# A gated recurrence with two dense layers on one core: all tasks in a new order, with 43 matmuls of zeros in place of 68

## The chip, the cores and the metric

One core of a Trainium2 chip runs the whole program in one launch. The metric is device time in microseconds, the median of the runs of the kernel: 453.35 us over 3 runs (452.59, 454.88 and 453.35). Engines are named as in the profile: PE is TensorE (PEld its weight loads), DVE VectorE, ACT ScalarE, POOL GpSimd, and SP is SyncE, whose queue issues the DMAs.

## What is computed

The first part is a recurrence over 768 steps for 2 x 8 heads of size 40, the second two dense layers of 1536 hidden columns over all 1536 tokens. Cut to its core:

```python
for t in range(S):
    m_new = np.maximum(f_gate[:, :, t] + m, i_gate[:, :, t])
    f_stab, i_stab = np.exp(f_gate[:, :, t] + m - m_new), np.exp(i_gate[:, :, t] - m_new)
    C = f_stab[..., None, None] * C + i_stab[..., None, None] * np.einsum('bhd,bhe->bhde', vt, kt)
    n = f_stab[..., None] * n + i_stab[..., None] * kt
    y[:, :, t] = sigmoid(o_gate[:, :, t]) * (C @ qt) / np.maximum(np.abs(n @ qt), 1.0)
x = y.transpose(0, 2, 1, 3).reshape(1536, 320)
x = (sigmoid(x @ w_gate) * (x @ w_val)) @ w_out
return ((x @ w_a) * (x @ w_b)) @ w_out2
```

## The kernel before, in words

The recurrence is cut into 12 steps of 64 time positions. A step s is a handful of tasks: kq and kv load its data (SP), E0 and E1 are two matmuls of the decay exponents (line 369) into a bank of the pool "e", X0 and X1 their Exp (ACT, L376), S the scores (L399, L414), P0 and P1 their product with the decays (DVE, L424), k0 and k1 the weighted keys (DVE or POOL, L379), ST and st the state sum (L433) and its copy (ACT), O the output sum (L443), N and M its normalisation, D, T, xh and xl the transposed copy of the result, split in a high and a low part, which the first layer reads. The output gate takes a Sigmoid (sg, ACT, L337), which needs another activation table than Exp.

Weights come as 24 blocks (w0 to w23, 960 KB each). Each is made narrow by na (ACT, L216 and L217), nb (DVE, L223), ns, nc and nd, and split by s1 (ACT), s2 (L256) and s3 (DVE or POOL).

The layers are cut into 84 units of one block of 128 hidden columns each. Units 0 to 23 work on 256 tokens and run between the steps of the recurrence; units 24 to 83 work on 512 tokens. A unit is ma and mb (its two products with the input, PE), ga_ (the activation, ACT, L598), gm (their product, DVE, L603), gh_ (ACT, L609) and gl_ (DVE, L614), which split it, and mm and mn, its product with the output weights (PE). In a wide unit ma is 8 pairs of matmuls of 512 columns side by side, mb 7 pairs, and mm and mn 6 pairs of 320 columns each (mm1_half and mm2_half, issued on line 549).

Four units make a segment: their mm and mn add to four sums, one for each 128 tokens, each in a PSUM bank of its own. Two of the banks are the whole pool "acc", two the whole pool "y" (BUFS, line 744), so the next segment's first mm must wait until the old sums are taken out by the four tasks ev (unit_evac: L700 on ACT, L702 and L704 on DVE). The first mm begins with the pair of the first sum of "acc" and the first of "y", and comes to the other two after three pairs. pick (line 899) gives the new sums their banks in the order in which the ev tasks of the old ones stand. In wide segments the four ev tasks read as evK.S, with K the segment and S the sum's block of 128 tokens; the first two of the four are of "acc", the last two of "y".

Nothing is reordered by a program: PLAN (from line 67) names all 1,298 tasks, and line 910 issues them in that order, so each engine runs its own tasks strictly in it. A letter behind a colon chooses the engine (V is DVE, G POOL, A ACT). A star and a number puts so many matmuls of zeros (fill, lines 169 to 172: 512 columns) on PE just ahead of the task: up to ma0 into a bank held for that, afterwards into the next bank that is taken. Waits are left to semaphores.

Of the kernel before, what the change touches and what calls it, by code (L numbers as in the profile page):

```python
# [73 lines left out]
P04 ma1 s12 M3:G k14:G gc2 gp0 D3 mb1 xl2 gm0 s32:G S5 T3 k04:V E05 st3 kv5 gh_0 xh3 O4 xl3 ga_1 X05 ST4 ma2  # L74
N4 pl3 s22:G E15 na3 gp1 P05 k05:G X15 w4 gm1 kq7 gl_0:V M4:V gh_1 mb2 nb3 ga_2 P15 ns3 gp2 ma3 k15:G st4 mb3
E16 gm2 gl_1:G mm0 kv7 nc3 X16 mm1 E07 E06 ma4 ga_3 ev0.0:V ev0.1:V nd3:V gh_2 X06 gp3 mb4 S6 E17 X07 D4 s13
gm3 S7 og2 ST5 O5 na4 k16:V gh_3 X17 P16 P06 gl_2:G k06:G nb4 mm2 s23:V N5 st5 ga_4 s33:G q17:V gp4 gl_3:G P07
ns4 pl4 mm3 sg2 gm4 ma5*1 k17:G mb5 M5:G nc4 O6*1 ST6 kv8 ev1.3:V P17 E18 ma6 ga_5 D5 ev1.2:V mb6 X18 E08
nd4:G gh_4 T5 X08 gp5 ma7 T4 gl_4:V gm5 xh5 kq8 gh_5 gl_5:G ga_6 q07:V mm4 xl5 xh4 N6 mb7 gp6 xl4 w5 st6 kv9
gm6 E19 mm5 kq9 S8 q18:G M6:G k18:G ev2.0 k07:V O7 ga_7 ST7 gh_6 gp7 P18 gm7 D6 na5 P08 N7 ma8 mb8 E09 ma9  # L80
gl_6:G nb5 ns5 ev2.1 nc5 X19 st7 gh_7 q08:G ga_8 M7:G gl_7:G mm6 gp8 T6 mb9 s14 nd5:V ma10 D7 mm7 gm8 s34:G
k08:G X09 T7 xh6 s24:V xh7 kq10 pl5 mb10 ev3.2 xl7 w6 q19:V ga_9 gh_8 gl_8:G q09:G k09:G s15 O8 S9 gp9 xl6 gm9
ev3.3 ST8 P19 N8 P09 ga_10 gh_9 st8 E111 ma11 mm8 mb11 gp10 k19:V O9 na6 ST9 E110 gm10 kq11 M8:G gl_9:G N9
ga_11 ma12 mm9 X110 gh_10 kv11 gp11 gl_10:V M9:V X111 D8 s35:V D9 gm11 nb6 mb12 E010 kv10 X010 k110:V ma13 T9
ga_12 mb13 gh_11 st9 s25:G mm10 T8 xh9 q010:V gp12 w7 gl_11:G gm12 xl9 xh8 ga_13 k010:V gp13 ma14 mm11 gh_12
ev4.4:A ev4.5:A mb14 gm13 gl_12:V q110:G ma15 xl8 ns6 ga_14 nc6 mm12 S11 gp14 gh_13 ST10 gm14 nd6:V P111 E011
gh_14 gl_13:G X011 mb15 ga_15 P011 q011:G st10 mm13 ma16 q111:V gp15 s16 S10 P010 P110 gm15 O11 gl_14:V mb16
N11 gh_15 ga_16 na7 O10 gp16 N10 mm14 ma17 mb17 M11:G D11 gm16 M10:V gl_15:V ma18 D10 s26:V gh_16 T11 mm15
ga_17 T10 mb18 gp17 xh11 gm17 gh_17 gl_16:G ma19 xh10 s36:V ev5.7:V ev5.6:A mb19 ga_18 xl11 mm16 xl10 gp18
gm18 gl_17:G mm17 ga_19 gh_18 ma20 k011:V gl_18:G nb7 mb20 gp19 ns7 gm19 nc7 ma21 gh_19 mm18 ga_20 gl_19:V  # L90
mb21 mm19 gp20 gm20 nd7:V ga_21 ma22 mb22 gh_20 gp21 gl_20:G gm21 w8 ma23 ev6.8:A gh_21 ga_22 gl_21:V ev6.9:V
gp22 gm22 s17 mb23 mm20 ga_23 na8 gh_22 gp23 gm23 mm21 s27:G ma24 s37:V nb8 ma25 mb24 mb25 gh_23 ns8 gl_23:G
# [5 lines left out]
s110 ma35 s310:G gh_32 mb34 ev9.7 s210:G ev9.4 na11 gh_33 ev9.5 gl_32 mm32 mb35 ga_34 mn32 nb11 ns11 gl_33
mm33 nc11 gm34 ga_35 gh_34 gm35 nd11:G gl_34 ma36 ma37 w12 mn33 s111 mm34 mb36 mn34 na12 nb12 ns12 s311:G mb37
s211:G gh_35 ga_36 gl_35 mm35 w13 nc12 gm36 ma38 ga_37 gm37 mn35 gh_36 mb38 nd12:V ev10.10 gl_36 ev10.9 ma39  # L100
ev10.8 gh_37 s112 s212:G ga_38 ev10.11 gm38 gl_37 mm36 na13 ma40 mn36 nb13 mm37 mb39 gh_38 mb40 mn37 gl_38
# [16 lines left out]
ma64 mn61 mb64 ga_63 nb21 gl_62 gm63 ma65 ns21 s120 nc21 gh_63 mm62 ga_64 gl_63 mb65 s320:V mn62 s220:G gm64  # L118
nd21:G ga_65 s121 gh_64 mm63 ma66 mn63 mb66 gm65 gl_64 s221:G ma67 ga_66 ev17.0 ev17.1 s321:G gm66 gh_65
ev17.2 ev17.3 w22 mm64 gl_65 na22 ma68 mn64 mb67 mm65 ga_67 mb68 gh_66 nb22 gm67 ma69 w23 mn65 ns22 gl_66 mm66  # L120
mb69 ga_68 gh_67 gl_67 nc22 nd22:G ga_69 gm68 gm69 mn66 mm67 ma70 mn67 gh_68 na23 ev18.4 ev18.5 gl_68 mb70
ma71 ga_70 ev18.7 ev18.6 gh_69 s122 nb23 mm68 gl_69 ns23 s222:V mb71 mn68 mm69 gm70 s322:V nc23 gh_70 ma72
# [910 lines left out]
```

## Time and profile before

| | |
|---|---|
| median of 3 runs | 453.35 us |
| the profiled execution | 453.09 us |
| its span, first to last instruction | 451.3 us |
| mean granted TensorE clock | 0.993 |
| PE busy, weight loads busy | 430.8 us, 395.0 us |
| DVE, ACT, POOL busy | 299.4, 261.5, 124.4 us |
| moved by DMA | 39.55 MB |

Busy times are unions of instructions. Matmul records are pipelined and their ends modelled, so a busy PE may still be held up for a short while; a wait is only seen as idle time of PE behind the modelled end.

### The profile page before, as it was taken

To read this page: it belongs to the slowest core of one execution; us is meant where nothing else is said; L and a number is where in the kernel's file an instruction comes from. 1 tells how busy PE (TensorE), PEld (TensorE's weight loads), DVE (VectorE), ACT (ScalarE), POOL (GpSimd) and SP (SyncE) were. 2 spreads that over 40 slices of the span, in tenths; PEclk is the share of its full clock that TensorE was granted. 3 is DMA by queue.
4 is the path that set the end of the run, shared out by engine and by line. 5 is a ranking of instruction groups with operands and counts; after the bars stand their busy time and mean duration, and the time that the engine had idled before them with its cause. 6 is when DMAs were issued, how large, how long until landed. Compare 5 with 4: busy or idle time off the path is not lost.

```text
span 451.3 us, 12061 instructions
## 1 busy us (share of the span) xinstructions
PE 430.8 (95%) x5116; PEld 395.0 (88%) x5116; DVE 299.4 (66%) x507; ACT 261.5 (58%) x471; POOL 124.4 (28%) x124
## 2 busy tenths in 40 slices
...
GB/s 223 286 235 295 81 197 285 99 126 63 82 8 89 7 84 18 93 155 1 73 104 56 34 88 1 89 89 1 89 89 1 97 80 2 1 1 2 1 60 116
DMA packets 10470, 39.55 MB, mean 88 GB/s; under 512 B 1840, under 2 KB 3760, under 8 KB 10416
## 3 DMA queue, kind: packets, MB, share of 16 engines
...
q10 hardware_dynamic: 288, 0.33, 0.2%
q14 instruction: 14, 0.11, 0.1%
...
## 4 chain that ended last, share of the span: by engine, by line
PE 82%; ACT 6%; DVE 6%; DMA 2%; issue 1%; POOL 1%; DVEq 0%; SPq 0%; ACTq 0%; POOLq 0%
PE acc L549 21%; PE pa L549 20%; PE pb L549 19%; PE pa L526 8%; PE sp L414 2%; DMA Y<-in_kv_dram 2%; PE o L443 2%; PE acc L533 1%; PE first L172 1%; PE st L433 1%; PE acc L535 1%; PE acc L534 1%; PE e L369 1%; DVE x2tok L704 1%; ACT gh L609 1%
## 5 line engine op out<-in xcount | busy, mean ns | idle before, releaser
L549 PE MATMUL pb<-xb,W 64*128 64x512 f32 x900 | 211.4, 379 | 0.0
L549 PE MATMUL pa<-xb,W 64*128 64x512 f32 x900 | 209.6, 379 | 0.0
L549 PEld LDWEIGHTS pa<-xb,W 64*128 64x128 f32 x900 | 162.9, 187 | 6.0 <-issue 0.2
L549 PEld LDWEIGHTS pb<-xb,W 64*128 64x128 f32 x900 | 163.5, 187 | 4.8
L549 PE MATMUL acc<-W,gh 64*128 64x320 f32 x960 | 108.5, 300 | 7.6 <-DVE x2tok L704 4.4
L549 PEld LDWEIGHTS acc<-W,gh 64*128 64x128 f32 x960 | 93.7, 186 | 13.2 <-DVE x2tok L704 6.1
L609 ACT ACTIVATE gh<-g 128x512 fp32r<-128x512 f32 (+1 forms) x84 | 47.4, 566 | 65.4 <-PE acc L549 54.0
L549 PE MATMUL acc<-W,gl 64*128 64x320 f32 x480 | 84.1, 297 | 0.0
L603 DVE TENSOR_TENSOR g<-g,pb 128x512 f32<-128x512 f32 x60 | 41.0, 687 | 60.1 <-ACT g L598 59.8
L598 ACT ACTIVATE g<-pa 128x512 f32<-128x512 f32 x60 | 35.7, 595 | 71.3 <-PE pa L549 68.8
L614 DVE TENSOR_TENSOR gl<-g,gh 128x512 fp32r<-128x512 f32 (+1 forms) x68 | 47.7, 704 | 42.5 <-ACT gh L609 42.3
L549 PEld LDWEIGHTS acc<-W,gl 64*128 64x128 f32 x480 | 58.8, 187 | 0.1
L256 POOL TENSOR_TENSOR W<-wst,W 128x832 fp32r<-128x832 f32 x14 | 28.7, 2050 | 100.0 <-ACT W L250 77.1
L526 PE MATMUL pa<-xb,W 128*128 128x256 f32 x384 | 48.7, 278 | 0.3 <-DVE ge L659 0.3
L526 PEld LDWEIGHTS pa<-xb,W 128*128 128x128 f32 x384 | 46.1, 192 | 1.2 <-DVE ge L659 0.6
L216 ACT ACTIVATE cva<-wst 128x960 f32<-128x960 f32 x24 | 31.5, 1311 | 6.0 <-DMA wst<-in_w_dram 2.6
L234 DVE SCALAR_TENSOR_TENSOR cva<-wst,cva 128x960 int32<-128x960 int32 x24 | 33.1, 1378 | 0.3
L704 DVE SCALAR_TENSOR_TENSOR x2tok<-acc,x2tok 128x320 f32<-128x320 f32 x52 | 22.9, 483 | 13.0 <-PE acc L549 12.8
L240 POOL TENSOR_TENSOR wst<-cva,wst 128x960 int32<-128x960 int32 x7 | 16.6, 2371 | 51.7 <-DVE cva L234 33.4
L217 ACT ACTIVATE wst<-wst 128x960 int32<-128x960 uint32 x24 | 30.6, 1276 | 0.0
L250 ACT ACTIVATE W<-wst 128x832 fp32r<-128x832 f32 x24 | 26.4, 1102 | 1.2 <-POOL wst L240 0.6
L614 POOL TENSOR_TENSOR gl<-g,gh 128x256 fp32r<-128x256 f32 x16 | 17.3, 1086 | 31.1 <-ACT gh L609 22.7
...
## 6 DMA issues: line engine op xcount, KB each, us to landing
...
rhsE<-V SPq DMA_DIRECT2D x24, 2.0 KB
```

The source lines that it names most:

```text
L216: nc.scalar.activation(cva[0], hi.bitcast(F32), AF.Abs)
L217: nc.scalar.activation(lo, lo.bitcast(U32), AF.Copy, scale=2.0**-29)
L234: nc.vector.scalar_tensor_tensor(ai, hi, -0x40000000, ai, op0=ALU.bitwise_and, op1=ALU.bitwise_or)
L250: nc.scalar.activation(w[:, 0:NH], g[:, 0:NH], AF.Copy)
L256: e.tensor_tensor(w[:, NH : 2 * NH], g[:, 0:NH], w[:, 0:NH].bitcast(F32), op=ALU.subtract)
L526: nc.tensor.matmul(dst, w[:, w0 : w0 + P], x[:, h, cb].rearrange("p a b -> p b a"), start=(i == 0), stop=(i == 7))
L549: last = [nc.tensor.matmul(o, w, x, start=st, stop=sp) for o, w, x, st, sp in pair]
L598: nc.scalar.activation(t, pa, AF.Copy if l else AF.Sigmoid)
L603: nc.vector.tensor_tensor(t, t, pb, op=ALU.mult)
L609: nc.scalar.activation(gh, g, AF.Copy)
L614: eng.tensor_tensor(gl, g, gh.bitcast(F32), op=ALU.subtract)
L704: nc.vector.scalar_tensor_tensor(dst[:, 0:DM], acc, half, dst[:, 0:DM], op0=ALU.mult, op1=ALU.add)
```

## The change

Only PLAN differs. The same 1,298 tasks stand in another order. The matmuls of zeros go from 68 (E00*25 S0*4 E01*5 S1*4 ST0*5 E14*3 T0*5 S3*7 O2*4 ST2*4 ma5*1 O6*1) to 43 (S0*14 E01*2 E11*2 S1*4 E02*5 E13*6 ST0*1 S3*3 ST2*3 ST4*1 E08*2). Some tasks change their engine: of k0 and k1 five go from DVE to POOL net, of nd three; one of gl_; two of M, two of the q tasks, one pr and one half of a split (s2 or s3) go from POOL to DVE net; and of the ev tasks three from ACT to DVE. In the queue of SP kq1 now stands ahead of kv0 and og0, and kv3 ahead of kv2. The lines of the diff around the start and around eight of the segments' ends:

```diff
-start yz0 cst lhs0:A ga0 gb0 gd0 rhs1:A ge0 gl1 ga1 rhs0:A yi0:A gc0 gb1 w0 pr0:V na0 E00*25 gd1 pr1:V nb0 E10
-X10 kq0 kv0 ge1 lhs1:A X00 og0 kq1 sg0 w1 ns0 k10:V gc1 S0*4 E11 yz2 yz1 gl2 pr3:G kq2 E01*5 nc0 X11 kv1 k00:G
-P10 P00 S1*4 X01 kq3 kv2 pr2:V E12 O0 X12 yi1:A nd0:V P01 P11 pr4:V ST0*5 E02 pr5:G E03 k11:G na1 S2 X02 k01:G
-st0 ga2 N0 nb1 og1 M0:V s10 P12 s30:G s20:V yi2:A k12:G k02:G w2 P02 O1 E13 ns1 ST1 N1 X03 nc1 gb2 X13 D0 M1:V
-nd1:V E14*3 T0*5 S3*7 kv3 st1 X14 sg1 kq4 gd2 kv4 kq6 k13:G k03:G P03 xh0 D1 P13 kq5 O2*4 s11 ST2*4 T1 na2 xl0
-s21:V E04 S4 st2 O3 N2 s31:G nb2 xh1 ge2 ST3 P14 w3 kv6 xl1 ma0 ns2 M2:G D2 X04 N3 nc2 T2 mb0 nd2:V xh2 ga_0
...
-gl_27 nb9 w10 mm26 mb29 mn26 ns9 mm27 nc9 ga_29 gm28 gm29 gh_28 ma30 mn27 nd9:V gh_29 na10 ma31 mb30 gl_29
-gl_28 ev8.0 ev8.3 ev8.2 nb10 ev8.1 s19 ga_30 ns10 mm28 mb31 gm30 nc10 mn28 mm29 s29:G gh_30 gl_30 ga_31 ma32
...
-mm38 ns13 ga_39 ga_40 nc13 gm39 gh_39 ma41 gl_39 gm40 mn38 mm39 gh_40 nd13:G s312:V ma42 mb41 mn39 mb42 gl_40
-w14 ev11.0 s113 ga_41 s213:G gm41 ev11.1 s313:G ga_42 gh_41 ev11.2 ev11.3 mm40 ma43 gm42 w15 yt0 na14 gl_41
...
-yh1 yl1 ga_44 s114 mm43 ma45 mn43 gm44 na15 gh_44 s214:G gl_44 ev12.7 mb45 s314:G ga_45 ma46 w16 ev12.6 ev12.5
-gm45 nb15 ev12.4 mm44 gh_45 ns15 yt2 gl_45 yh2 yl2 nc15 mb46 ga_46 gm46 mn44 nd15:V ma47 yt3 yh3 na16 yl3 mm45
...
-nc16 mb49 w17 yh4 yl4 ga_49 mn46 gm49 gh_48 yt6 mm47 ma50 mn47 yh6 gl_48 yl6 nd16:V yt5 ev13.10 ev13.8 yh5
-mb50 yl5 ga_50 gm50 s116 gh_49 k111:V ev13.9 ev13.11 mm48 s216:V ma51 yt7 yh7 na17 gl_49 mn48 yl7 gh_50 mb51
...
-gm52 ma53 yh8 gh_52 yl8 mn51 gl_52 nc17 mb53 ev14.1:A ga_53 ma54 nd17:V ev14.0:V ev14.3:V gm53 na18 ev14.2:V
-gh_53 gl_53 mm52 nb18 yt11 mb54 mn52 yh11 yl11 mm53 ga_54 s117 s217:G gm54 yt9 ma55 mn53 yh9 mb55 ns18 yl9
...
-gh_56 na19 ma58 gm57 mn55 gl_56 ev15.6:A gh_57 nb19 ev15.5:A mb58 ns19 ev15.4:A s118 ga_58 ev15.7:A nc19 ma59
-gm58 mm56 mb59 gl_57 ga_59 s218:V ma60 mn56 nd19:G s318:G gh_58 w20 mm57 gm59 gl_58 s119 mb60 mn57 gh_59 ga_60
-gl_59 s319:G gm60 na20 mm58 s219:G ma61 mn58 mm59 ma62 mn59 gh_60 mb61 ev16.9:A ga_61 gl_60 nb20 ns20 nc20
-gm61 gh_61 gl_61 ev16.11:V mb62 ev16.8:V ev16.10:A nd20:V ga_62 w21 mm60 ma63 gm62 mn60 na21 mm61 gh_62 mb63
...
-gh_74 ga_75 gm75 mm73 mb76 mn73 ma77 gl_74 gh_75 ga_76 mm74 gm76 mb77 mn74 gl_75 mm75 ma78 mn75 gh_76 ga_77
-gm77 gh_77 ev20.0 gl_77 gl_76 ev20.3 ma79 ev20.2 mb78 ga_78 gm78 ev20.1 mm76 mb79 mn76 ga_79 gh_78 mm77 ma80
...
+yz1 start ga0 gl1 ga1 gb0 gb1 gd0 yz2 yz0 cst lhs0:A yi1:A rhs0:A ge0 w0 gd1 gc0 kq0 na0 kq1 ge1 kv0 pr0:V
+pr1:V lhs1:A nb0 yi0:A S0*14 ns0 E10 X10 nc0 gc1 nd0:V E00 w1 X00 E01*2 P00 P10 k00:G gl2 E11*2 rhs1:A k10:G
+pr2:V X01 X11 na1 pr3:V kq2 S1*4 ga2 E12 gb2 nb1 s10 og0 kv1 og1 X12 E02*5 X02 E13*6 ST0*1 O0 P11 s20:V sg0
+P01 s30:G ns1 k11:G k01:G N0 E03 S2 kq3 gd2 st0 M0:G pr4:G O1 ST1 kv3 kv2 yi2:A sg1 P02 kq4 w2 X03 P12 k12:G
+N1 S3*3 D0 T0 nc1 M1:V X13 st1 P03 k02:V ge2 E04 P13 nd1:V k13:G xh0 X04 D1 kv4 ST2*3 s11 O2 k03:V s31:G S4
+s21:G xl0 pr5:V E14 st2 T1 X14 O3 xh1 kq5 N2 xl1 P14 ST3 kv5 E05 kq7 M2:V N3 k04:G na2 k14:G ma0 nb2 D2 mb0
...
+gl_26 mb28 mm26 s19 gh_27 na10 ga_28 ma29 gl_27 nb10 gm28 mn26 mm27 gh_28 mb29 ns10 ga_29 mn27 nc10 gm29 gl_28
+ev8.0 ev8.3 ma30 s29:V ma31 nd10:G ev8.1 mb30 gh_29 ga_30 s39:G ev8.2 s110 gl_29 mm28 mb31 mn28 ga_31 gm30 w11
...
+mm37 ma40 ma41 mb40 nd13:G mn37 gl_38 mm38 ga_40 w14 gh_39 gl_39 mb41 mn38 gm40 mm39 ga_41 s113 ma42 gh_40
+gm41 s313:V mn39 mb42 na14 gl_40 s213:V ev11.3 nb14 gh_41 ev11.1 ev11.2 ns14 ev11.0 ma43 ga_42 gm42 mm40 mb43
...
+mb44 ga_44 yt2 mn42 gm44 s314:G yh2 gh_44 gl_44 s214:V mm43 ma45 mn43 na15 yl2 ev12.4 mb45 ma46 ev12.7 ga_45
+ev12.6 nb15 w16 ns15 ev12.5 mm44 gm45 yt3 nc15 mb46 mn44 gh_45 yh3 yl3 nd15:V ma47 gl_45 ga_46 gm46 s115 mm45
...
+gl_47 w17 nc16 mb49 mn46 mm47 ga_49 gh_48 gm49 yl4 gl_48 nd16:G yt6 mn47 na17 yh6 ma50 ev13.10 ev13.8 ev13.9
+gh_49 ev13.11 mm48 gl_49 yl6 nb17 mb50 ga_50 mn48 yt5 mm49 yh5 s116 gm50 ma51 yl5 ns17 yt7 s316:G mn49 gh_50
...
+gl_51 yt8 s217:V mn50 yh8 mb53 yl8 gh_52 yt11 mm51 k011:V ga_53 s317:V yh11 gl_52 mn51 gm53 yl11 ev14.1:V
+ev14.3:V yt9 ma54 na18 ev14.2:V ev14.0:A yh9 mm52 w19 nb18 ns18 gh_53 yl9 nc18 mb54 nd18:G mn52 ga_54 gl_53
...
+s218:V gl_55 gm56 mb57 mn54 mm55 ga_57 gh_56 ma58 mn55 s318:V gm57 ma59 ev15.6:V mb58 w20 mb59 gh_57 gl_56
+ev15.7:V ev15.4:V ga_58 gl_57 ev15.5:A mm56 ga_59 nd19:V na20 gm58 ma60 mn56 mm57 gh_58 mb60 gm59 ma61 mn57
+gl_58 mm58 mb61 mn58 s119 s319:G nb20 ga_60 gh_59 ns20 gl_59 gm60 mm59 ga_61 ma62 gm61 s219:G gh_60 w21 gl_60
+mn59 ev16.11:A mb62 ev16.8:V nc20 ev16.9:A ga_62 ev16.10:A gh_61 ma63 mm60 mb63 gm62 gl_61 nd20:G mn60 na21
...
+gl_73 mb75 mm73 mb76 ga_75 gh_74 gl_74 gm75 mn73 mm74 gh_75 ma77 ga_76 mn74 gl_75 gm76 gh_76 mb77 ga_77 mm75
+ma78 gm77 mn75 ev20.3 ev20.1 ev20.0 mb78 ev20.2 gl_76 ga_78 gh_77 out3 gm78 ma79 gl_77 mm76 mb79 mn76 gh_78
...
```


## Rows read from the trace of the kernel before

**Rows 1.** Windows by stage: length, busy us (instructions) per engine, PEclk, DMA share, GB/s

```profile
9.80:28.50 18.70, 15.27 (x262) 9.76 (x262) 17.40 (x29) 17.16 (x27) 9.82 (x10) 1.00 0.98 253
28.50:41.40 12.90, 12.90 (x243) 8.78 (x237) 11.78 (x23) 12.03 (x21) 6.15 (x8) 1.00 0.94 307
41.40:134.90 93.50, 92.33 (x1278) 87.89 (x1274) 81.63 (x161) 77.78 (x179) 48.95 (x49) 1.00 0.38 122
134.90:445.60 310.70, 303.08 (x3325) 285.77 (x3324) 180.83 (x274) 149.04 (x238) 55.85 (x52) 0.99 0.16 53
```

**Rows 2.** Waits of PE from 134.9 to 445.6 us: total, times, longest

```profile
PE acc L549 <- DVE x2tok L704: 4.4, 4, 1.8
PE acc L549 <- DVE x2tok L702: 2.0, 2, 1.7
PE acc L549 <- ACT x2tok L700: 0.9, 1, 0.9
```

**Rows 3.** Groups of instructions: xcount, busy us, mean ns of one, idle before and releasers

```profile
L549 PE MATMUL acc<-W,gh 64*128 64x320 f32 x960 | 108.5, 300 | 7.6 <-DVE x2tok L704 4.4 <-DVE x2tok L702 2.0 <-ACT x2tok L700 0.9
...
L614 DVE TENSOR_TENSOR gl<-g,gh 128x512 fp32r<-128x512 f32 (+1 forms) x68 | 47.7, 704 | 42.5 <-ACT gh L609 42.3
...
L216 ACT ACTIVATE cva<-wst 128x960 f32<-128x960 f32 x24 | 31.5, 1311 | 6.0 <-DMA wst<-in_w_dram 2.6 <-DVE wst L240 1.9 <-POOL wst L240 1.2
...
L704 DVE SCALAR_TENSOR_TENSOR x2tok<-acc,x2tok 128x320 f32<-128x320 f32 x52 | 22.9, 483 | 13.0 <-PE acc L549 12.8 <-PE acc L535 0.2
...
L223 DVE TENSOR_SCALAR cva<-cva 128x960 f32<-128x960 f32 x24 | 16.9, 703 | 8.0 <-ACT cva L216 7.9
...
L337 ACT ACT_TABLE_LOAD x3 | 3.8, 1283 | 0.1
...
L256 DVE TENSOR_TENSOR W<-wst,W 128x832 fp32r<-128x832 f32 x10 | 11.4, 1141 | 0.0
```

**Rows 4.** Chain that ended last, 268 to 272 us: start us, us, what

```profile
268.21 0.61 ACT g L598
...
268.84 0.69 DVE g L603
...
269.53 0.40 DVE Kw L379
...
269.93 0.41 DVE x2tok L704
...
270.39 1.56 PE acc L549 x6
```

**Rows 5.** Window just behind that wait, PE alone: busy (instructions), PEclk

```profile
270.80:274.20 3.40, 3.40 (x18) 0.50 0.02 5
```

**Rows 6.** Windows of line 172, the matmuls of zeros, on PE: busy (instructions)

```profile
9.80:28.50 18.70, 4.58 (x18) 1.00 0.98 253
28.50:41.40 12.90, 5.82 (x23) 1.00 0.94 307
```

**Rows 7.** Timeline of the first 30 us: start us, us, instruction, idle before

```profile
1.17 7.22 PE L172 MATMUL first<-zb 128*128 128x512 bf16 x25 [1.17 <-DVE zb L176]
...
2.42 0.15 PEld L172 LDWEIGHTS <-zb 128*128 128x128 bf16 x1 [0.27 <-issue]
...
2.85 0.15 PEld L172 LDWEIGHTS <-zb 128*128 128x128 bf16 x1 [0.28 <-issue]
...
9.87 0.70 PE L369 MATMUL e<-rhsE,lhsE 128*128 128x512 f32 x2 [1.47 <-DVE lhsE L349]
...
12.58 0.65 PE L399 MATMUL sp<-kq,cs 40*64 40x512 f32 x2 [1.13 <-DMA kq<-in_kqT_dram]
...
19.15 1.07 PE L443 MATMUL o<-Y,Z 128*64 128x41 f32 x30
...
26.13 0.32 PE L414 MATMUL sp<-kq 40*64 40x64 f32 x2 [2.03 <-issue]
...
28.18 0.33 SPq L209 DMA_DIRECT2D wst<-in_w_dram  x1
```

More of the change, by code (lines that the diff above doesn't have):

```diff
@@ L73 @@
-s21:V E04 S4 st2 O3 N2 s31:G nb2 xh1 ge2 ST3 P14 w3 kv6 xl1 ma0 ns2 M2:G D2 X04 N3 nc2 T2 mb0 nd2:V xh2 ga_0
[L74 to L92, printed above, removed]
@@ L98 @@
[L98 to L101, printed above, removed]
-mm38 ns13 ga_39 ga_40 nc13 gm39 gh_39 ma41 gl_39 gm40 mn38 mm39 gh_40 nd13:G s312:V ma42 mb41 mn39 mb42 gl_40
@@ L103 @@
-w14 ev11.0 s113 ga_41 s213:G gm41 ev11.1 s313:G ga_42 gh_41 ev11.2 ev11.3 mm40 ma43 gm42 w15 yt0 na14 gl_41
-mn40 mm41 mb43 yh0 gh_42 yl0 ga_43 mn41 nb14 ns14 gl_42 ma44 gm43 nc14 mm42 yt1 gh_43 mb44 mn42 nd14:G gl_43
-yh1 yl1 ga_44 s114 mm43 ma45 mn43 gm44 na15 gh_44 s214:G gl_44 ev12.7 mb45 s314:G ga_45 ma46 w16 ev12.6 ev12.5
-gm45 nb15 ev12.4 mm44 gh_45 ns15 yt2 gl_45 yh2 yl2 nc15 mb46 ga_46 gm46 mn44 nd15:V ma47 yt3 yh3 na16 yl3 mm45
-nb16 gh_46 mb47 ma48 ga_47 s115 gm47 mn45 gl_46 ns16 s315:G gh_47 mb48 gl_47 ga_48 gm48 ma49 s215:V mm46 yt4
@@ L118 @@
[L118 to L122, printed above, removed]
@@ L128 @@
-ev21.6 ev21.4 gh_81 out1 ga_82 ev21.7 ev21.5 mm80 ma83 mn80 gm82 gl_81 mm81 out7 mb83 mn81 out5 gh_82 ga_83
-out3 gl_82 gm83 mm82 gh_83 gl_83 mn82 mm83 mn83 ev22.8 ev22.9 out9 ev22.10 ev22.11 out11
+yz1 start ga0 gl1 ga1 gb0 gb1 gd0 yz2 yz0 cst lhs0:A yi1:A rhs0:A ge0 w0 gd1 gc0 kq0 na0 kq1 ge1 kv0 pr0:V
+pr1:V lhs1:A nb0 yi0:A S0*14 ns0 E10 X10 nc0 gc1 nd0:V E00 w1 X00 E01*2 P00 P10 k00:G gl2 E11*2 rhs1:A k10:G
+pr2:V X01 X11 na1 pr3:V kq2 S1*4 ga2 E12 gb2 nb1 s10 og0 kv1 og1 X12 E02*5 X02 E13*6 ST0*1 O0 P11 s20:V sg0
@@ new lines @@
+w4 gl_1:V ns3 mm1 E06 E07 gp2 ma4 mb4 gm2 nc3 ga_3 X07 nd3:V E17 ev0.0:V ev0.1:V k15:G X06 O5 S6 S7 gh_2 gp3
+s13 X17 gm3 q07:V gl_2:G gh_3 ga_4 s33:G N5 s23:V P06 na4 ST5 gl_3:G M5:G gp4 ma5 mb5 P16 gm4 st5 kv6 pl4 P17
+nb4 ga_5 P07 mm2 E18 k16:G og2 kv7 gh_4 D5 mm3 ma6 X18 E08*2 sg2 ns4 k06:G gp5 M4:V ev1.3:V gm5 ev1.2:V O6
+gl_4:G D4 X08 ST6 nc4 kq8 nd4:V w5 kv9 kv8 st6 ma7 mb6 T5 mm4 N6 gh_5 T4 mb7 ga_6 xh4 M6:V gl_5:V xh5 xl4 kq10
+gp6 q17:G k07:G k17:G gm6 s14 ga_7 O7 ST7 xl5 E19 mm5 ma8 E09 gh_6 na5 s24:V ev2.0 gp7 mb8 X19 gm7 q08:G
```

43 lines of the change are left out of this document (35 added, 8 removed).

## The prediction, made before the change was run

> **What bounds the kernel now.** I read the windows by stage first. From 28.5 us on PE is busy practically without a break: 12.90 of 12.90 us up to the first unit (ma0, at 41.4), 92.33 of 93.50 us up to the first wide unit (ma24, at 134.9), 303.08 of 310.70 us up to the last matmul (445.6) [rows 1]. But the early stage has other claims on it: DVE is busy for 11.78 and ACT for 12.03 of the 12.90 us before ma0, the DMA engines for 0.94 of them, and 23 of PE's matmuls there are of zeros, 5.82 us of recorded time [rows 1, 6]. So PE is full there partly because it was given filler, and DVE and ACT set the pace. In the wide stage it is the reverse: DVE and ACT are busy for 180.83 and 149.04 of 310.70 us, and PE alone decides [rows 1].
>
> Then the waits of PE in the wide stage. There are seven, 7.3 us in all, and every one is "acc" waiting for an evacuation of x2tok, by L704, L702 or L700 [rows 2]: the first mm of a segment waits until an old sum has left its bank. PE starts late for no other reason that the profile names.
>
> The chain of waits shows how such a wait is made. At the end of segment 13 the old order gives DVE the tasks ev13.10, ev13.8, yl5, gm50, k111, ev13.9, ev13.11. gm50 cannot start before ga_50, and ga_50 not before mb50, the last thing on PE ahead of mm48. So the last two sums leave their banks only after activation 0.61, product 0.69, weighted keys 0.40 and the first of the two evacuations 0.41 us, while PE stands still in the middle of mm48 until 270.39 [rows 4]. Behind it PE's granted clock is 0.50, the 1.2 GHz level, for 3.40 us [rows 5].
>
> **The change part by part.** The sum is made against the profiled execution, 453.09 us, whose span is 451.3 us; the median of the runs shown is 0.26 us above it.
>
> *The waits at segments' ends: what they cost.* Recorded waits, 4.4 + 2.0 + 0.9 = 7.3 us [rows 2]. Each wait begins behind a modelled end: a matmul of 320 columns is recorded with 300 ns [rows 3], but six pairs of them take about 0.84 us. (A wide unit takes 303.08 / 60 = 5.05 us [rows 1] for 15 pairs of 512 and 12 of 320 columns, 11,520 in all, 0.44 ns a column.) So a pair keeps PE for 0.14 us, and each wait hides 0.16 us more: 7 x 0.16 = 1.1 us. The stretch at half clock loses half of its 3.40 us, 1.7 us. Together 10.1 us, the most that this part can give.
>
> *What is left of it.* I went through every boundary of the wide stage in the new order, with the evacuation (0.48 us), the weight tasks on DVE (0.70 and 1.14 us) and gl_ (0.70 us) in their queue [rows 3]. ma and mb take about 1.8 and 1.6 us by the same 0.44 ns a column. At mm28, mm44, mm56, mm60 and mm76, where the old order has an evacuation behind a task that itself waits for PE, the new one has at least one sum of "acc" and one of "y" leave first, and nothing that waits for the last mb stands ahead of the rest. At mm48 the four stand together on DVE, ahead of mb50 altogether: 4 x 0.48 = 1.9 us beside ma50's 1.8 and half of mm48; I count 0.2. Two boundaries look worse than before. At mm40 DVE has gl_40 and s213 (0.70 + 1.14) ahead of the four, and nb14 and ns14 (about 0.70 each) between them; the fourth leaves about 4.3 us after mn39, mm40 needs it after mb42, ma43 and half of itself, 1.6 + 1.8 + 0.4 = 3.8: some 0.5 to 0.7. At mm52 it depends on how late POOL delivers block 17: 0 to 0.9, I take 0.5. With 0.3 for the others the rest is 1.7 us, so this part gives 10.1 - 1.7 = **8.4 us**; bounds 3 (as many new waits as a bad reading of the queues could leave) and 10.1.
>
> *The matmuls of zeros.* Ahead of the first real matmul 25 become 14; both end long before data is there (25 end at 8.39, E00 starts at 9.87 [rows 7]), so 11 of the 25 that go cost nothing. From 9.8 us to ma0 there were 18 + 23 = 41 [rows 6]; now 26. After ma0 2 become 3. If the early stage were bound by PE, 15 x 512 columns x 0.44 ns = 3.4 us would come back. It isn't, by the DVE and ACT shares above: the two had 1.1 and 0.9 us of slack in the 12.90 [rows 1]. I take nothing for them alone, and keep 3.4 as the other end.
>
> *The new start.* PE's first task is now S0, which waits for kq0 as before (12.58 [rows 7]); kq0 is fifth in SP's queue in both. E10 and E00, which ran at 9.87, come behind it. X10 and X00 so start some 3 us later, after which ACT has na1 (2.6 us with both halves [rows 3]) and s10 ahead of X12. E13 needs the bank that X12 frees, and stands on PE ahead of ST0 and O0: O0 moves from 19.15 [rows 7] to about 25. kv3 waits for O0 on SP, with kv2, kq4 and w2 queued behind it; w2 was issued at 28.18 [rows 7] anyhow, kv2 is issued some 10 us later than it was, and by my walk through the queues ST2 and O2, two steps on, still find it. Against this, the tasks of DVE and ACT ahead of ma0 are nearly the same ones (N3, M2 and X04 come in, nb2 goes), and sg0 and sg1 now follow each other without an Exp between them, which saves two table loads of 1.28 us [rows 3] on ACT. DVE, which starts on the step's work about 1 us later but then has it waiting, reaches xl1 and so ma0 at about 41 instead of 41.4: **0.5 us** gained; bounds 3.4 gained (above) and 6 lost (O0's delay carried through).
>
> *From ma0 to ma24* the same PE work stands in another order (1.2 us of 93.5 idle before [rows 1]): 0, bounds -2 and +3. *Engines changed:* DVE loses and POOL gains about 2 us over the whole span, ACT loses three evacuations; POOL works 55.85 of 310.70 us in the wide stage [rows 1], and the weights that it makes are due several units later. That cover gone, a nd on POOL instead of DVE would delay one block by 1 us. *The tail* behind mn81 has the same order on PE, DVE and ACT; the outputs out1 to out7 only trade places ahead of it: 0.
>
> Sum: -8.4 - 0.5 = -8.9 us, 444.2 by the profiled execution, **444.5 us** by the median.
>
> **A rule that speaks against it.** After the first fillers PE is now idle from about 5.8 to 12.6 us. The trace has waits of 1.47, 1.13 and 2.03 us in the first 30 us [rows 7] inside windows whose clock stayed 1.00 [rows 1], and one of 1.8 us [rows 2] with 3.40 us at 0.50 behind it [rows 5]; at the start the fillers' weight loads are 0.43 us apart [rows 7], the 1.2 GHz pace. So I count S0 and the E matmuls behind it at the low level, about 1.5 us that ACT and DVE mostly don't see. The Trainium skill, TensorE: Matmul & The Clock Gate, section "HAM oscillation — how this bites in real kernels", says that a PE which idles between bursts falls back to its throttled clock each time; the trace agrees for one wait and not for three. By the rows the sum stands; the price if the rule held throughout is the last rival.
>
> **The rivals.**
> - *The fillers are on the path.* The chain passes through them before ma0. Then 3.4 us more: 441. Against it, DVE and ACT at 91 and 93% there [rows 1].
> - *O0's delay is carried to ma0.* 5 to 6 us of the gain go: 450. For it: one strict queue on each engine, with E13 ahead of ST0 and O0, and kv2 behind kv3. Against it: DVE then has a stock of work, and the old order lost 2.03 us in S2 for no data [rows 7].
> - *The order doesn't do what it says:* as the banks come free earlier, other tasks on DVE or ACT are late, and the waits return as waits for gl_ or for a bank of "mm1" or "e"; 0 to 2 us gained, 452. Against it: mm has 6.5 us or more of PE work between mb and itself in nearly every wide unit, in both orders, for a chain of four instructions of 0.6 to 0.7 us each [rows 3, 4].
> - *Slower: PE stays at 1.2 GHz before ma0.* Up to ma0 PE has 15.27 + 12.90 - 4.58 - 5.82 = 17.8 us of real work [rows 1, 6] and 26 fillers, 5.9 us. At half clock 23 us become 46 or 47, ma0 comes at 12.6 + 46.4 = 59, and the total is 453 + 18 - 8.4 = 463. It decides once PE does more than some 16 of the 23 us at the low level (11 us lost, less 5 of slack taken up). Against it: after 3.40 us at 0.50 the clock was back, in a stretch without a pause [rows 5].
>
> **How the numbers follow.** Forecast 0.58 (440 to 448), fillers on the path 0.12, O0's delay 0.12, waits return 0.10, low clock 0.08. The range takes the forecast's own, 441 and 450, and the near end of the waits that return: 438 to 451. About 0.5% (2.3 us) can be told from no change, as the three runs lie 2.3 us apart. Faster: 0.58 + 0.12 + most of 0.12 = 0.80; same: the returned waits and a little, 0.11; slower: 0.09.
>
> **What would show it.** Right: PE's waits for x2tok in the wide stage fall from 7.3 to below 2 us, the stretch from ma24 to the last matmul is 301 to 304 us, no window there is below 1.00 in clock, and ma0 starts at 39 to 43 us with O0 near 25. Wrong: waits at mm40 or mm52 of over 1 us; PE waiting for gl or for pa and pb banks; a granted clock of 0.50 over most of 12 to 40 us; ma0 behind 45.

## The result, and the profile after

The changed kernel takes 440.14 us (median of 4 runs, 436.93 to 442.26) against 454.12 (452.59 to 455.81): 0.9685 of the time before [0.9613, 0.9757], or 14.0 us less. Forecast were 444.5 us, range 438 to 451: faster, as said, and by more than the forecast. The profiled execution of after took 442.26 us (span 440.5), the slowest of its four runs. Three of the kernels below (no fillers, 34 at S0, before with 51) had one execution each that lay over 1.5% above the fastest of its kernel and is left out of their medians; of the first two it is the profiled one.

The windows of after by stage, cut at ma0, ma24 and the last matmul (columns as in [rows 1]):

```profile
9.80:28.50 18.70, 17.19 (x200) 10.01 (x200) 18.23 (x31) 17.93 (x27) 6.13 (x7) 0.80 0.87 250
28.50:43.90 15.40, 15.38 (x282) 11.76 (x281) 11.19 (x23) 9.27 (x20) 9.85 (x11) 0.69 0.74 219
43.90:136.10 92.20, 91.25 (x1277) 86.92 (x1275) 81.07 (x160) 79.81 (x179) 47.93 (x52) 1.00 0.41 128
136.10:434.70 298.60, 298.31 (x3325) 284.82 (x3324) 175.07 (x274) 149.71 (x235) 56.19 (x52) 1.00 0.17 55
```

Against [rows 1]: up to ma0 43.9 instead of 41.4 us (+2.5), ma0 to ma24 92.2 instead of 93.5 (-1.3), ma24 to the last matmul 298.6 instead of 310.7 (-12.1). With 0.1 more in the tail that is -10.8, the difference of the two spans. The whole gain of this execution lies in the wide stage, where PE is now idle for 0.3 us instead of 7.6 and the clock stays at 1.00.

All waits of PE in after, over the whole span (total, times, longest):

```profile
PE sp L399 <- DMA kq<-in_kqT_dram: 5.0, 1, 5.0
PE first L172 <- DVE zb L176: 1.2, 1, 1.2
PE sp L399 <- DVE Z L424: 0.5, 1, 0.5
PE tp L485 <- ACT Dt L376: 0.4, 1, 0.4
PE e L369 <- DVE xb L498: 0.2, 1, 0.2
PE sp L414 <- ACT Dt L376: 0.2, 1, 0.2
```

No line says x2tok: the 7.3 us of [rows 2] are gone, and nothing has come in their place. How that looks at segment 13, the place of [rows 4], is in after's timeline of DVE and PE (start us, us, instruction, idle before):

```profile
262.87 1.68 DVE L704 SCALAR_TENSOR_TENSOR x2tok<-acc,x2tok 128x320 f32<-128x320 f32 x4
265.82 0.69 DVE L614 TENSOR_TENSOR gl<-g,gh 128x512 fp32r<-128x512 f32 x1 [1.27 <-ACT gh L609]
...
267.96 0.69 DVE L603 TENSOR_TENSOR g<-g,pb 128x512 f32<-128x512 f32 x1 [0.34 <-ACT g L598]
...
264.80 0.43 PE L549 MATMUL acc<-W,gh 64*128 64x320 f32 x4
265.07 0.30 PE L549 MATMUL acc<-W,gl 64*128 64x320 f32 x2
265.20 0.43 PE L549 MATMUL acc<-W,gh 64*128 64x320 f32 x4
```

The four sums leave their banks in one run of 1.68 us, while PE is busy with ma50, and gm50 (L603) comes 3.4 us behind them; mm48 (at 264.80) goes through in one piece. Before, gm50, which waits for the last PE task ahead of mm48 (mb50), stood in front of the third and fourth; now mb50 itself stands behind mm48.

The start is less tidy. After's windows cut where its clock changes:

```profile
10.90:17.70 6.80, 6.80 (x47) 3.83 (x45) 6.64 (x10) 6.43 (x12) 2.51 (x2) 0.50 1.02 286
17.70:27.90 10.20, 9.64 (x147) 5.51 (x146) 9.96 (x18) 9.80 (x15) 3.49 (x5) 1.00 0.74 213
27.90:38.10 10.20, 10.18 (x131) 6.99 (x127) 7.81 (x16) 5.25 (x11) 5.75 (x6) 0.50 0.89 259
```

PE ran at a granted clock of 0.50 (1.2 GHz) for 17.0 us ahead of ma0. The first stretch stands behind the wait of 5.0 us for kq0; the second behind one in which PE was busy for 9.64 of 10.20 us.

### The profile page after: what moved, and what is told of

Same layout as the page of the kernel before. It is cut to its first block, busy times and chain, and to the rows that moved or that the text cites. A ratio compares the mean times of both kernels' runs of the same rounds, so it can differ in the third digit from the quotient of the medians.

```text
span 440.5 us, 12010 instructions
## 1 busy us (share of the span) xinstructions
PE 426.8 (97%) x5091; PEld 395.1 (90%) x5091; DVE 292.8 (66%) x505; ACT 261.5 (59%) x466; POOL 123.7 (28%) x127
## 4 chain that ended last, share of the span: by engine, by line
PE 84%; DVE 5%; DMA 4%; ACT 3%; SPq 2%; issue 1%; DVEq 0%
PE pa L549 23%; PE acc L549 22%; PE pb L549 21%; PE pa L526 6%; PE sp L414 2%; PE o L443 2%; DMA wst<-in_w_dram 1%; SPq L362 1%; DMA og<-in_ogate_dram 1%; PE acc L533 1%; PE st L433 1%; PE acc L535 1%; PE acc L534 1%; DMA gates<-in_gates_dram 1%; PE tp L485 1%
## 5 line engine op out<-in xcount | busy, mean ns | idle before, releaser
L549 PE MATMUL pb<-xb,W 64*128 64x512 f32 x900 | 209.1, 377 | 0.0
L549 PE MATMUL acc<-W,gh 64*128 64x320 f32 x960 | 104.8, 298 | 0.3
L549 PEld LDWEIGHTS acc<-W,gh 64*128 64x128 f32 x960 | 91.5, 186 | 2.8 <-SPq L545 1.0
L549 PE MATMUL acc<-W,gl 64*128 64x320 f32 x480 | 80.2, 296 | 0.0
L603 DVE TENSOR_TENSOR g<-g,pb 128x512 f32<-128x512 f32 x60 | 41.0, 684 | 56.1 <-ACT g L598 55.9
L549 PEld LDWEIGHTS acc<-W,gl 64*128 64x128 f32 x480 | 53.9, 186 | 0.1
L240 POOL TENSOR_TENSOR wst<-cva,wst 128x960 int32<-128x960 int32 x10 | 23.2, 2317 | 79.5 <-DVE cva L234 70.9
L260 POOL TENSOR_TENSOR W<-wst,W 64x128 fp32r<-64x128 f32 x18 | 10.7, 595 | 84.2 <-ACT W L251 64.8
L217 ACT ACTIVATE wst<-wst 128x960 int32<-128x960 uint32 x24 | 32.5, 1352 | 0.0
L234 DVE SCALAR_TENSOR_TENSOR cva<-wst,cva 128x960 int32<-128x960 int32 x24 | 30.3, 1261 | 0.2
L704 DVE SCALAR_TENSOR_TENSOR x2tok<-acc,x2tok 128x320 f32<-128x320 f32 x52 | 22.8, 481 | 10.9 <-PE acc L549 10.9
L250 ACT ACTIVATE W<-wst 128x832 fp32r<-128x832 f32 x24 | 28.6, 1191 | 1.7 <-DVE wst L240 1.6
L614 POOL TENSOR_TENSOR gl<-g,gh 128x256 fp32r<-128x256 f32 x17 | 16.4, 967 | 32.6 <-ACT gh L609 18.7
```

Source lines behind the costliest of these rows:

```text
L217: nc.scalar.activation(lo, lo.bitcast(U32), AF.Copy, scale=2.0**-29)
L234: nc.vector.scalar_tensor_tensor(ai, hi, -0x40000000, ai, op0=ALU.bitwise_and, op1=ALU.bitwise_or)
L240: e.tensor_tensor(lo, cva[0].bitcast(I32), lo, op=ALU.add)
L250: nc.scalar.activation(w[:, 0:NH], g[:, 0:NH], AF.Copy)
L549: last = [nc.tensor.matmul(o, w, x, start=st, stop=sp) for o, w, x, st, sp in pair]
L603: nc.vector.tensor_tensor(t, t, pb, op=ALU.mult)
```

## The experiments

The theory: (a) some 11 us of the gain are banks that the sums leave in time, which hangs on a few tasks around seven segments' ends; (b) the new start and the middle give 2 us or less; (c) the number of fillers decides nothing. Rivals: the start or the fillers give a larger share; the new order of everything is needed; the slow clock at the start costs several us.

### The two halves of the order, one at a time

The order of before up to ma24 and the changed one behind it, then the other way round (each against the changed kernel; here and below a diff shows pieces of PLAN's lines):

```diff
-yz1 start ga0 gl1 ga1 gb0 gb1 gd0 yz2 yz0 cst lhs0:A yi1:A rhs0:A
+start yz0 cst lhs0:A ga0 gb0 gd0 rhs1:A ge0 gl1 ga1 rhs0:A yi0:A
...
 ma24 s37:G ma25
```

> The old order up to ma24, then all that is left in the new order; 68 matmuls of zeros, since all of the old ones lie ahead of ma24. Theory (the gain is that of the wide stage, the new start gives none): ma24 at 134.9 us as before, the stretch from ma24 to the last matmul about 298 us instead of 310, about 441 us, ratio 0.974; no 0.50 clock before 134 us. Rival (the new start and the fewer fillers share in the gain): less than 9 us under the kernel before.

```diff
-ma24 s37:G ma25 gm23 s27:V gh_23 mb24 gl_23:V
+ma24 s37:V ma25 mb24 mb25 gh_23 gl_23:G
...
```

> The new order up to ma24, then what is left in the old order. Theory: the waits for x2tok in the wide stage are all back (7 us recorded), the stretch from ma24 to the last matmul about 310 us, and the time is that of the kernel before within 2 us, ratio 0.996 to 1.005. Rival (the start shares in the gain): 3 us or more under the kernel before.

With the old start: 445.97 us, 0.9796 [0.9724, 0.9867]. With the new start alone: 450.78 us, 0.9916 [0.9878, 0.9953]. So the changed order from ma24 on gives some 9 us (6 to 12.5) in spite of a seam, and the new start with the middle 2.1 to 5.5. Both expectations missed: 441 us was expected of the first, and of the second no change beyond 2 us, so part (b) of the theory was put too low.

The old start with the new rest, its wide stage, the stretch behind the seam, and two of its waits of PE:

```profile
134.50:437.70 303.20, 301.02 (x3325) 277.58 (x3324) 177.58 (x275) 149.78 (x235) 57.44 (x53) 0.99 0.16 55
146.40:149.80 3.40, 3.40 (x18) 2.72 (x16) 2.63 (x6) 2.96 (x5) 0.00 (x0) 0.50 0.00 0
...
PE acc L533 <- ACT gh L609: 1.0, 1, 1.0
PE acc L535 <- DVE gl L614: 0.9, 1, 0.9
```

No wait for x2tok; but the two orders don't fit at ma24. Two products on DVE and ACT come late there for mm22 and mm23 (1.0 + 0.9 us), and 3.40 us at half clock behind them cost some 1.7: an estimated 3.6 us that are the seam's. Without it the wide stage would take 299.6, one more than after's. In the kernel with the new start and the old rest the three waits of [rows 2] are back to a tenth (waits of PE from ma24 to the last matmul), and the stage takes 310.4 us:

```profile
PE acc L549 <- DVE x2tok L704: 4.4, 4, 1.8
PE acc L549 <- DVE x2tok L702: 1.9, 2, 1.7
PE acc L549 <- ACT x2tok L700: 0.9, 1, 0.9
```

### The evacuations alone, moved as early as they can stand

The order of before; in seven segments (8, 12 to 16, 20) the four ev tasks go right behind the segment's last mn, all on DVE. Segment 13:

```diff
-ma50 mn47 yh6 gl_48 yl6 nd16:V yt5 ev13.10 ev13.8 yh5 mb50 yl5 ga_50 gm50 s116 gh_49 k111:V ev13.9 ev13.11 mm48
+ma50 mn47 ev13.8 ev13.10 ev13.9 ev13.11 yh6 gl_48 yl6 nd16:V yt5 yh5 mb50 yl5 ga_50 gm50 s116 gh_49 k111:V mm48
```

> The old order with one thing moved: at the ends of the seven segments 8, 12, 13, 14, 15, 16 and 20 the four evacuations stand right behind the segment's last mn, on DVE, the first sums of acc and y ahead of the second. Theory (the waits come from the place of the evacuations in the queues, not from the rest of the order): PE's waits for x2tok fall from 7.3 to about 1 us, no 0.50 clock at 271 us, 443 us, ratio 0.973 to 0.982. Rival (only the whole new order avoids them; four evacuations in a row make gm and gl late and the wait returns as one for gl or for a pa or pb bank): at most 4 us under the kernel before.

455.99 us, 1.0019 [0.9991, 1.0046]: no gain at all. The theory as it was put had fallen. The wide stage, its waits of PE, and the timeline of DVE and PE at segment 13:

```profile
138.20:449.60 311.40, 303.30 (x3325) 281.08 (x3324) 184.49 (x281) 146.36 (x231) 56.81 (x52) 1.00 0.16 53
...
PE pb L549 <- DVE g L603: 3.0, 3, 1.8
PE t2mm L723 <- DVE xb L737: 2.3, 1, 2.3
PE t2e L723 <- DVE g L603: 1.1, 1, 1.1
PE pb L549 <- SPq L545: 0.6, 2, 0.4
PE acc L549 <- DVE gl L614: 0.5, 1, 0.5
...
269.85 1.68 DVE L704 SCALAR_TENSOR_TENSOR x2tok<-acc,x2tok 128x320 f32<-128x320 f32 x4 [2.68 <-PE acc L549]
...
272.05 0.35 DVE L737 TENSOR_TENSOR xb<-t2mm,xb 128x192 fp32r<-128x192 f32 x1
...
272.54 0.24 PE L723 MATMUL t2mm<-cs,x2tok 64*128 64x64 f32 x1 [2.32 <-DVE xb L737]
```

The x2tok waits are gone here too, but others of 7.5 us in all have come, and the stage is as long as before. DVE now stands still for 2.68 us until mn47 gives it the first sum, with gl_48 and yl6 (L737) queued behind the four. yl6 frees the banks that yt5 needs, and yt5 stands on PE ahead of mb50: PE waits 2.32 us for it. In other segments gm_ is held instead, and PE waits for the bank of pb. Here an evacuation too early in its engine's queue costs what one too late costs. The changed kernel has the four behind mn47 as well, but there gl_48 stands ahead of them, DVE comes to them without a pause (262.87), and yt5 stands on PE behind mm48.

### One wait put back

The changed kernel with mb50, ga_50 and gm50 ahead of the last two sums, the pattern of before at one place:

```diff
-ma50 ev13.10 ev13.8 ev13.9 gh_49 ev13.11 mm48 gl_49 yl6 nb17 mb50 ga_50 mn48 yt5 mm49 yh5 s116 gm50 ma51
+ma50 ev13.10 ev13.8 mb50 ga_50 gm50 ev13.9 gh_49 ev13.11 mm48 gl_49 yl6 nb17 mn48 yt5 mm49 yh5 s116 ma51
```

> The new order with mb50, ga_50 and gm50 moved ahead of ev13.9, as the old order had it. Theory: PE stands still in mm48 for 1.4 to 2 us, with or without a stretch at half clock behind it (up to 1.7 us more); the window from ma48 to ma56 is 2 to 4 us longer than the 42.8 us of the new order. Rival (something else sets this stretch): under 0.5 us longer.

One run, 443.97 us. Its wait, mm48 in PE's timeline, and the window from ma48 to ma56 here and in after:

```profile
PE acc L549 <- DVE x2tok L704: 1.4, 1, 1.4
...
265.68 0.30 PE L549 MATMUL acc<-W,gl 64*128 64x320 f32 x2
267.38 0.93 PE L549 MATMUL acc<-W,gh 64*128 64x320 f32 x4 [1.41 <-DVE x2tok L704]
...
249.10:294.80 45.70, 44.00 (x500) 39.14 (x498) 28.23 (x54) 25.21 (x46) 12.75 (x11) 1.00 0.19 66
...
250.40:293.20 42.80, 42.70 (x498) 39.84 (x496) 28.41 (x54) 25.21 (x46) 12.30 (x11) 1.00 0.21 71
```

The wait returns, at the same task, and from ma48 to ma56 the kernel takes 45.70 us where after takes 42.80 (and its repeat 42.85): 2.9 us for a recorded wait of 1.4. The granted clock stayed at 1.00 here.

### The queue mended at seven segments' ends, nothing else

The order of before with fewer than 20 of the 1,298 tasks moved: at the ends of segments 8, 12 to 16 and 20 the late ev tasks go ahead of the tasks that wait for PE or are long, but no further. Three of the places:

```diff
-gl_29 gl_28 ev8.0 ev8.3 ev8.2 nb10 ev8.1
+ev8.0 ev8.3 ev8.1 ev8.2 gl_28 gl_29 nb10
...
-mb50 yl5 ga_50 gm50 s116 gh_49 k111:V ev13.9 ev13.11 mm48
+mb50 yl5 ga_50 ev13.9 ev13.11 gm50 s116 gh_49 k111:V mm48
...
-ev20.0 gl_77 gl_76 ev20.3 ma79 ev20.2 mb78 ga_78 gm78 ev20.1
+ev20.0 ev20.3 ev20.1 ev20.2 gl_76 gl_77 ma79 mb78 ga_78 gm78
```

> The old order with only the queue around the eight late evacuations mended, each past those tasks alone that wait for PE or are long: ev8 ahead of gl_28 and gl_29, ev12 ahead of gl_44 and gm45, ev13.9 and ev13.11 ahead of gm50 and k111, ev14.0, ev14.3 and ev14.2 ahead of nd17 and gm53, ev15.7 ahead of s118, ev16.10 ahead of ga_61 and gh_61 and ev16.11 and ev16.8 ahead of gm61, ev20 ahead of gl_77, gl_76 and gm78; unlike in the run where the evacuations stood right behind mn, nothing that is ready earlier is put behind them. Theory (each wait is made by what stands between the evacuations in the queue): PE's waits in the wide stage fall under 1.5 us, the stretch from ma24 to the last matmul is 298 to 301 us, 443 to 445 us, ratio 0.975 to 0.980. Rival (waits of the old order can't be mended without a new order of everything, as the run with evacuations right behind mn suggests): less than 4 us under the kernel before.

444.48 us, 0.9788 [0.9756, 0.9819]: 9.6 us less than before, about 70% of the whole change's gain. Its wide stage, and DVE at segment 13:

```profile
137.50:437.80 300.30, 299.95 (x3325) 281.97 (x3324) 180.73 (x275) 149.41 (x237) 55.79 (x52) 1.00 0.16 55
...
267.94 0.88 DVE L704 SCALAR_TENSOR_TENSOR x2tok<-acc,x2tok 128x320 f32<-128x320 f32 x2
269.24 0.69 DVE L603 TENSOR_TENSOR g<-g,pb 128x512 f32<-128x512 f32 x1 [0.42 <-ACT g L598]
```

PE has no recorded wait in this stage, and DVE does the two evacuations in the time in which gm50 could not start anyway. 300.3 us is within 1.7 of after: the place of the evacuations relative to the tasks that wait for PE is the cause, and this part of the gain needs no new order of all tasks.

### The fillers and the slow clock at the start

The changed kernel again as it is, with 89 matmuls of zeros, with none, and with 34 ahead of S0 alone; the kernel before with 51 instead of 68. The counts of the kernel with 89 against those of the changed one, and further down those of before that differ:

```diff
-S0*14 E01*2 E11*2 S1*4 E02*5 E13*6 ST0*1 S3*3 ST2*3 ST4*1 E08*2
+S0*34 E01*4 E11*4 S1*4 E02*5 E13*6 ST0*1 O0*2 ST1*3 S3*7 T0*5 E04*3 ST2*4 O2*4 ST4*1 E08*2
```

> The new order, unchanged, beside the next three on one chip. All theories: 437 to 443 us, ratio about 0.969, with one or two stretches of 7 to 10 us at a granted clock of 0.50 before ma0, and ma0 between 40 and 44 us by how long they are.

> The new order with 89 matmuls of zeros instead of 43, all 46 more of them before ma0 (S0 34, E01 4, E11 4, O0 2, ST1 3, S3 7, T0 5, E04 3, ST2 4, O2 4). Theory (what the new start loses, it loses to stretches at half clock, half of their length each): the granted clock stays at 1.00 from about 5 us to the end, ma0 comes at 40 us or earlier in every run, the runs lie within 2 us of each other, and the median is 2 to 4 us under the new order's. Rival (PE is full before ma0, so each filler costs its 0.22 us): the 26 that are added behind S0's cost 4 to 6 us, ma0 at 46 or later.

> The new order without any matmul of zeros. Theory: the granted clock is 0.50 for most of 10 to 40 us, ma0 at 45 to 50 us, the median 3 to 8 us above the new order's. Rival (fillers only cost): 2 to 4 us under the new order's.

> The new order with S0*34 instead of S0*14 and nothing else: 20 more matmuls of zeros, all of them before the first data is there. Theory (zeros are free where PE has nothing to do, and cost where it has): the half clock from 11 to 18 us is gone, S0 takes 1.4 instead of 2.3 us, and the median is 0 to 2 us under the new order's 439.6 to 440.1. Rival (DVE and ACT hide PE's clock before ma0 altogether): no difference within 0.3%.

```diff
-E14*3 T0*5 S3*7 O2*4 ST2*4
+E14*1 T0*1 S3*2 O2*1 ST2*1
```

> The old order with 51 matmuls of zeros instead of 68: of the 23 between 28.5 us and ma0 6 are left, as in the new order (E14 1, T0 1, S3 2, O2 1, ST2 1). Theory (DVE and ACT set the pace there, and zeros keep the clock): no gain, 0 to +3 us, ma0 at 41 to 44 us. Rival (the fillers are on the path): ma0 at 38 us and 3 to 4 us under the kernel before.

Medians: the changed kernel again 439.55 us (0.9708 [0.9664, 0.9752]), 89 fillers 441.33 (0.9745 [0.9718, 0.9772]), with none 440.20 (0.973 [0.9695, 0.9765]), 34 at S0 441.62 (0.9707 [0.9663, 0.9751]); before with 51 453.44, 0.9998 [0.9966, 1.0029]. None of the expectations for other fillers in the changed kernel held in full: more gained nothing, and with none neither 3 to 8 us were lost nor 2 to 4 won. That for before with 51 (no gain, ma0 at 41 to 44) held.

Why, in the windows up to ma0 of the kernel with 89, in the first of them and one output sum of the kernel with none, and in the last of them of before with 51:

```profile
9.80:28.50 18.70, 17.50 (x250) 10.41 (x250) 18.20 (x33) 17.98 (x27) 7.87 (x9) 1.00 0.90 258
28.50:42.30 13.80, 13.80 (x265) 9.63 (x264) 8.98 (x20) 8.83 (x20) 7.85 (x9) 1.00 0.77 235
```

```profile
9.80:28.50 18.70, 15.24 (x177) 11.00 (x178) 18.01 (x33) 17.89 (x28) 7.59 (x8) 1.00 0.88 246
...
36.66 1.92 PE L443 MATMUL o<-Y,Z 128*64 128x41 f32 x32
```

```profile
28.50:42.30 13.80, 11.48 (x214) 9.24 (x213) 12.56 (x26) 12.30 (x20) 5.53 (x8) 0.76 0.95 308
```

With 89 the clock never falls ahead of ma0, but PE is then full (13.80 of 13.80 us) and ma0 starts at 42.3. With none, S0 takes 2.4 us instead of 1.4 (with 89), and PE shows the low level's durations up to about 38 us (the output sum at 36.66 takes 1.92 us, the next one 1.13), though the profile gives the clock as 1.00 there; ma0 starts at 42.8. (From 38.8 us on that profiled execution ran at a granted clock of 0.95, and is not read further.) From 9.8 to 28.5 us DVE is busy for 18.0 to 18.2 of 18.7 us in both, whatever PE's clock. In before with fewer fillers PE is idle instead, and DVE and ACT are nearly as busy as they were (91 and 89%): the fillers were in the gaps. What these runs show is a sum: fewer fillers give PE room and more time at half clock (0.76 in the last window), and the two were not taken apart.

### The saved table loads undone

```diff
-O1 ST1 kv3 kv2 yi2:A sg1 P02 kq4 w2 X03 P12
+O1 ST1 kv3 kv2 yi2:A P02 kq4 w2 X03 sg1 P12
```

> The new order with sg1 moved behind X03, so that an Exp stands between the two Sigmoids again and two more activation tables of 1.28 us are loaded before ma0. Theory (ACT is one of the two engines that set the pace of the start, so the two loads saved are a part of what the start gained): ma0 1 to 2.6 us later, the median 1 to 2.6 us above the new order's. Rival (DVE alone sets the pace): under 0.7 us.

440.03 us, 0.9682 [0.9653, 0.9712]: two table loads more (8 in all instead of 6), and no time that can be told from after; the 1 to 2.6 us expected to be lost did not come.

## Why the prediction was right, and where its terms were not

**The wide stage: mechanism right, term too small** (8.4 us forecast, 12.1 measured). The signs came: no x2tok wait (forecast below 2 us), no window below 1.00, and the stage at 298.6 us even beat the 301 to 304. It repeats: from the start of its first matmul to that of its last it is 298.4 us in after and 298.4 to 299.5 in four later profiles with this order, 310.3 in before and 310.0 with the new start alone. Two steps were mis-sized.

First, the bound of 10.1 us, called the most that this part can give. I gave each recorded wait 0.16 us of hidden time, as if PE waited once. Two banks are awaited at each place, one by the first pair and one by the fourth, and a wait shorter than a modelled end leaves no record at all. In PE's timeline of before at mm44:

```profile
244.28 0.38 PE L549 MATMUL pb<-xb,W 64*128 64x512 f32 x1
244.68 0.54 PE L549 MATMUL acc<-W,gh 64*128 64x320 f32 x4
245.02 0.33 PE L549 MATMUL acc<-W,gl 64*128 64x320 f32 x2
246.15 0.54 PE L549 MATMUL acc<-W,gh 64*128 64x320 f32 x4 [0.80 <-DVE x2tok L704]
```

Pairs of 512 columns follow each other every 0.21 or 0.22 us; here 0.40 pass from the last pair to the first of mm44, 0.19 us lost with no wait named. From the start of mm44 at 244.68 three pairs of 0.14 us end at 245.10, and the fourth starts at 246.15: 1.05 us, of which the profile names 0.80. Until the next task starts, at 246.66, mm44 takes 1.98 us, 1.16 more than six pairs need. By the same reading mm28 loses 0.69, mm48 2.66, mm52 0.52, mm56 1.18, mm60 2.13 and mm76 1.79: with mm44 10.1 us where 7.3 are recorded (I had 8.4). The half clock costs 1.36 more (I had 1.7). That is 11.5, against 0.3 at one place in after (at mm51): 11.2 of the 12.1.

Second, the 1.7 us of waits that I thought would remain, at mm40 and mm52 above all. None is there. After's timeline of DVE at mm40:

```profile
223.10 0.69 DVE L614 TENSOR_TENSOR gl<-g,gh 128x512 fp32r<-128x512 f32 x1 [0.32 <-ACT gh L609]
223.71 1.10 DVE L256 TENSOR_TENSOR W<-wst,W 128x832 fp32r<-128x832 f32 x1
224.74 0.47 DVE L704 SCALAR_TENSOR_TENSOR x2tok<-acc,x2tok 128x320 f32<-128x320 f32 x1
...
227.06 0.47 DVE L704 SCALAR_TENSOR_TENSOR x2tok<-acc,x2tok 128x320 f32<-128x320 f32 x1
```

mn39 starts at 223.49 and needs 0.82 us, so it is done at 224.3. I charged gl_40 and s213 (1.84 us) behind that; DVE had both begun before it, and only 0.4 us of them lay behind. The fourth sum leaves at 227.53, 3.2 us after mn39 and not 4.3; mm40 starts at 227.54. The walk through the queues counted durations and not how far ahead of PE the engine was.

**The start** (-0.5 us forecast). S0 waited for kq0, and O0 ran at 24.01 us (forecast about 25), as after's timeline shows:

```profile
10.75 1.06 PE L399 MATMUL sp<-kq,cs 40*64 40x512 f32 x2 [4.99 <-DMA kq<-in_kqT_dram]
...
24.01 1.10 PE L443 MATMUL o<-Y,Z 128*64 128x41 f32 x32
```

ma0 came at 43.9 (39 to 43 forecast), and one sign of being wrong came too: 15.9 of the 28 us from 12 to 40 ran at 0.50. But that depends on the execution: in the five profiled executions with the whole new start (after; new start alone; one wait put back; again; table loads) it was 43.9, 40.3, 42.9, 41.2 and 42.0, mean 42.1; in the four with the old start and its 68 fillers 41.4, 41.0, 44.5 and 43.5, mean 42.6. So -0.5 on the mean, as forecast, but the executions lie up to 3.6 us apart: that it agrees is luck, and no single profile could have shown it. Within each order ma0 goes with the time at half clock ahead of it: new 6.8 us of it with 40.3 and 41.2, 10.2 with 42.0, 11.9 with 42.9, 17.0 with 43.9; old none with 41.4 and 41.0, 6.8 with 44.5 and 43.5. At equal low-clock time the new start is some 3 us earlier (40.7 against 44.0 at 6.8 us); it is at half clock more often, and gives that back. This is read from few executions, and the pauses told of at the end are mixed into it.

**The middle** (0 forecast, bounds -2 and +3): 91.7 to 93.3 us in the same five, mean 92.3, against 93.5 to 94.0, mean 93.7: -1.4. Start and middle together -1.9, just below the interval of the new start alone (2.1 to 5.5); which task gives the middle's part stays open. With the wide stage's 12.1 that makes 14.0, as much as lies between the medians; in the repeat the wide stage gave 10.9 (299.8 us) and the ratio 13.2 us in all.

**The fillers at nothing:** right as a net of room and clock, by three counts of them and by before with 51.

**The rivals.** Fillers on the path (441): near the measured time by chance; the runs with 0, 51 and 89 don't show its 3.4 us. O0's delay: O0 came 4.9 us later and ma0 on the mean not at all. Waits that return: not in this order, but that is what the evacuations moved alone did, where x2tok's waits came back as waits for t2mm, t2e and pb. PE at 1.2 GHz ahead of ma0 (463): the mechanism exists, its price was wrong. I let every us lost by PE beyond 5 reach ma0. With no fillers PE was, by its durations, at the low level for nearly the whole start, and the median rose by 0.1 us over after's (0.7 over its repeat): fillers left out give PE room, and by the busy shares DVE and ACT pace the first 28.5 us. The Trainium skill, TensorE: Matmul & The Clock Gate, section "HAM oscillation — how this bites in real kernels", ties the fall of the clock to idle gaps between bursts of matmuls. After's wait of 4.99 us with 6.80 us at 0.50 behind it agrees. The stretch from 27.90 us does not: it stands behind one with 9.64 us busy of 10.20, there is no such gap ahead of it in the trace, and the trace decides.

**No version beat the changed kernel:** the best others lie at 440.03 and 440.20, within its own spread.
